# Fused pooled attention and gated feed-forward: the first block's turned probabilities move into buffers of the second tile's x, and the first tile's turns and value products move to other PSUM buffers

## The chip, the cores and the metric

The kernel runs on one core of one Trainium2 chip. The metric is the device time of one execution in microseconds (us). The engines of that core are named as the profile names them: PE does matrix products (PEld loads their stationary operand), DVE, ACT and POOL are the vector, scalar and general engines, and SP issues the transfers. Each engine works through its own list of instructions in the order in which the program gave them, and waits where an operand or a buffer is not ready.

## The reference

Inputs are q, k, v of 8 batches, 8 heads, 576 rows, 64 columns, and three weight matrices of a feed-forward layer with 512 inputs and 1536 inner columns.

```python
k_p = k.reshape(B, H, Sp, 8, D).mean(axis=3)      # 576 keys pooled to 72
v_p = v.reshape(B, H, Sp, 8, D).mean(axis=3)
scores = scale * np.matmul(q, k_p.transpose(0, 1, 3, 2))
scores = scores - np.max(scores, axis=-1, keepdims=True)
attn = np.exp(scores)
attn = attn / (np.sum(attn, axis=-1, keepdims=True) + 1e-09)
attn_out = np.matmul(attn, v_p)
x = attn_out.transpose(0, 2, 1, 3).reshape(B * S, H * D)   # 4608 x 512
a = x @ w_a
b = x @ w_b
return a * b @ w_out
```

The host hands the weights over as 64-bit floating point words, and the kernel turns them into float32 on the chip. Every operand of a product is split into a high and a low part, so that one product is three matmuls (high by high, high by low, low by high).

## The kernel before, in words

**Tiles, chunks and blocks.** The 4608 rows are nine tiles of 512. The attention works in chunks of at most 128 rows that belong to one batch. Chunks 0 to 3 are the first tile (the code calls them first, `i < early`), chunks 4 to 8 are the second tile. Chunks whose value product is made together form a block: chunks 0 and 1 are block 0, chunks 2 and 3 block 1, chunk 4 block 2, chunks 5 and 6 block 3, chunks 7 and 8 block 4.

**One chunk** (`chunk(i)`) goes through these stages, each after the one before: split q into qh and ql; the scores in two groups (`psc`, lines 407 to 424), of which DVE takes the maximum away (lines 401 and 402); the exponential on ACT (451); sum, a small addition and the reciprocal on DVE (453 to 455); the product with the reciprocal on POOL or DVE (457); the split into `pr` and `rem`, whose high part ACT copies (466, 468) and whose low part POOL makes (470, 471); three turns (`turn(0)`, `turn(1)`, `turn(2)`, the transposes of line 502 into `ptr`), each copied by ACT into the tiles p0, p1, p2 (503). The last chunk of a block then makes the value product in two halves (`po`, lines 537 to 546): ACT copies the result to xh (548) and DVE makes xl (550, shown under line 182, as every low part is).

**The feed-forward.** For a tile t and an inner slice f of 128 columns, `ffn_in(t, f)` is 24 matmuls: 12 into `psa` and 12 into `psb`; ACT copies psa to h (606), DVE multiplies it with psb (556), and h is split into hh and hl. `ffn_out(t, f)` is 12 matmuls into the four `acc` tiles. The weights of slice f must have been converted before (`convert_weights`: lines 224 and 225 on ACT, 226, 230 and 235 on DVE, for a, b and o) and split (`split_weight`). The order of slices is written out: in(0,0), in(0,1), out(0,0), in(0,2), out(0,1), in(0,3), out(0,2), in(0,4), in(1,4), out(0,3) and so on: from slice 4 the second tile's products share the first tile's weights.

**What sets the order around the change.** All the work beside the feed-forward consists of generators, the chains, that a small planner (`Chains`) resumes in steps while the program is being written. A chain that yields a number comes back so many steps later; one that yields `PE` joins a queue (`wanting`) and is resumed when it is granted its PE work. A queue entry with a lower rank goes first, and the rank of a chunk is its number. Three things set how fast steps and grants go:

- `need(ready)` runs steps one after the other until a condition holds, with up to 4 grants in each (`GROUPS`), and no matmul of the feed-forward is written between them. At the start it waits for all value products of the first tile and the first weights; before each `ffn_in(t, f)` it waits for `have(t)`, all value products of tile t.
- `ffn_in` makes one step before every 6 matmuls (4 in all) and `ffn_out` one before every 6 (2 in all), each with a single grant. After the first `ffn_in` there is one step more.
- A chain also waits for marks. Chunk i splits its rows into `pr` only after chunk i - 2 is turned; it turns only after chunk i - 1 is turned and the block before its own has its value product, since p0, p1 and p2 exist once (line 505). The scores of chunk i follow `probs` of chunk i - 2, and chunks of the second tile load their q after the scores of chunk i - 2.

The second tile's chunks start at fixed steps (14, 17, 20, 23, 26), whatever the feed-forward does. The conversion of slice f + 1 waits until `ffn_in(0, f - 1)` has begun; that of o starts with the first `ffn_in`.

**PSUM.** The tag `att` has two buffers, `acc` four, `psa` and `psb` one each. In the first tile the scores use `acc`, the turns `att`, the value product of block 0 `psa` and `psb`, and that of block 1 `att`. The scores and turns of the second tile use `att`.

Of the kernel before, what the change touches and what calls it, by code (L numbers as in the profile page):

```python
# [9 lines left out]
F32 = mybir.dt.float32  # L10
F32R = mybir.dt.float32r
# [9 lines left out]
P = 128  # L21
DM = H * D
DF = 1536
NT = 512
NTILE = B * S // NT
NF = DF // P
NK = DM // P
# [25 lines left out]
BLOCK, BLOCK_LATER = 256, 384  # L53
# [26 lines left out]
class Chains:  # L80
# [12 lines left out]
    def wait(self, *marks):  # L93
        while not all(m in self.done for m in marks if not isinstance(m[-1], int) or m[-1] >= 0):
            yield 1
# [26 lines left out]
def attn_moe_kernel(ctx: ExitStack, tc: tile.TileContext, q, k, v, vr, wa, wb, wo, out):  # L122
    nc = tc.nc
    const = ctx.enter_context(tc.tile_pool(name="const", bufs=1))
    sb = ctx.enter_context(tc.tile_pool(name="sb", bufs=2))
    ps = ctx.enter_context(tc.tile_pool(name="ps", bufs=1, space=bass.MemoryType.PSUM))
# [3 lines left out]
    mark, wait, done = chains.mark, chains.wait, chains.done  # L130
# [21 lines left out]
    tile_of = [(b * S + o) // NT for b, o, n in flat]  # L152
# [22 lines left out]
        start = stop  # L175
    block_of = [x for x, block in enumerate(blocks) for _ in block]
    vrems, parts, xtiles, turned, begun, later = {}, {}, {}, {}, [], {}
    upcoming = {name: [] for name in ("a", "b", "o", "h")}
    held = dict.fromkeys(upcoming, 0)

    def low_part(eng, lo, src, hi):
        eng.tensor_tensor(out=lo, in0=src, in1=hi.bitcast(F32), op=ALU.subtract)  # L182
# [188 lines left out]
    def chunk(i):  # L371
        b, o, n = flat[i]
        t, col = divmod(b * S + o, NT)
        first, soon = i < early, t < 2
# [19 lines left out]
        s = sb.tile([P, H, SP], F32, tag="s", name=f"s_{i}")  # L394
# [11 lines left out]
        if i < SUMMED:  # L406
            for g0 in range(0, NK, 2):
                yield from wait(("keys", b, g0))
                yield PE
                if first:  # L410
                    pt = ps.tile([P, 512], F32, tag="acc", name=f"psc_{i}_{g0}", bufs=4)
                else:
                    pt = ps.tile([P, 512], F32, tag="att", name=f"psc_{i}_{g0}", bufs=2)
                for j in range(2):
                    g = g0 + j
# [9 lines left out]
        else:  # L425
            for g in range(NK):
# [3 lines left out]
                pt = ps.tile([P, 512], F32, tag="att", name=f"psc_{i}_{g}", bufs=2)  # L430
# [45 lines left out]
        j = block_of[i]  # L476
# [6 lines left out]
        def turn(x):  # L483
            rows = P if x < 2 else NR
            num = NK if x < 2 else NG
            if x not in turned[j]:
                if tile_of[i] < 2:
                    turned[j][x] = sb.tile([P, num, BLOCK], F32R, tag=f"p{x}", name=f"p{x}_{j}", bufs=1)
                elif x == 0:
                    both = sb.tile([P, 2, NK, BLOCK_LATER], F32R, tag="work", name=f"p_{j}", bufs=1)  # L490
                    turned[j].update({0: both[:, 0], 1: both[:, 1]})
                else:
                    turned[j][x] = sb.tile([P, NK * BLOCK], F32R, tag="p0", name=f"p{x}_{j}", bufs=1)[
                        :, :NG * BLOCK_LATER
                    ].rearrange("p (g s) -> p g s", g=NG)
            dst = turned[j][x]
            pt = ps.tile([P, 512], F32, tag="att", name=f"ptr_{i}_{x}", bufs=2)
            ptr = pt.bitcast(F32R).rearrange("p (g s) -> p g s", g=NK)
            for g in range(num):
                src = pr[:n, x, 2 * g:2 * g + 2, :] if x < 2 else rem[:n, g]  # L500
                src = src.rearrange("p a s -> p (a s)") if x < 2 else src.rearrange("p a c s -> p (a c s)")
                nc.tensor.transpose(ptr[:rows, g, :n], src, ident[:n, :n])  # L502
            nc.scalar.copy(dst[:rows, :, c0:c0 + n], ptr[:rows, :num, :n])

        yield from wait(("turned", i - 1), ("value", j - 1))
        if t >= 2:
            yield from wait(*(("weight", name, NF - 1) for name in ("a", "b", "o")))
        for x in range(3):
            if x < 2 or t < 2:
                yield PE  # L510
            turn(x)
            if x != 1 or t < 2:
                yield 1
# [7 lines left out]
        xh, xl = xtiles[t]  # L521
# [3 lines left out]
        th, tl, tr = (turned[j][x] for x in range(3))  # L525
        for g0 in range(0, NK, per):
            yield PE
            if j == 0:
                po = ps.tile([P, 512], F32, tag="psb" if g0 else "psa", name=f"po_{j}_{g0}")
            else:  # L530
                po = ps.tile([P, 512], F32, tag="att", name=f"po_{j}_{g0}", bufs=2)
            pov = po[:, :per * total].rearrange("p (g s) -> p g s", g=per)
            for g in range(g0, g0 + per):
                if per == NK and g == NK // 2:
                    yield PE
                dst = pov[:, g - g0, :]
                nc.tensor.matmul(dst, vd[:, g, 0, :], th[:, g, :total], start=True, stop=False)
                nc.tensor.matmul(dst, vd[:, g, 0, :], tl[:, g, :total], start=False, stop=False)  # L538
                nc.tensor.matmul(dst, vd[:, g, 1, :], th[:, g, :total], start=False, stop=False)  # L539
                nc.tensor.matmul(  # L540
                    dst,
                    vrem[:NR, g // 2, g % 2].rearrange("p e d -> p (e d)"),
                    tr[:NR, g // 2, :total],
                    start=False,
                    stop=True,
                )
            gs = slice(g0, g0 + per)
            nc.scalar.copy(xh[:, gs, cols], pov)
            yield 1
            low_part(nc.vector, xl[:, gs, cols], pov, xh[:, gs, cols])  # L550
# [58 lines left out]
    acc = {}  # L609
# [52 lines left out]
    for kind, t, f, *_ in order:  # L662
        x = t * NF + f
# [7 lines left out]
    with tc.manual_schedule():  # L671
# [8 lines left out]
        for i in range(early):  # L680
            chains.start(chunk(i), (CHUNKS[0], i), EARLY_GAP * i)
        for i in range(early, sum(t < 2 for t in tile_of)):
            chains.start(chunk(i), (CHUNKS[0], i), SECOND_START + SECOND_GAP * (i - early))
# [15 lines left out]
        for n, (kind, t, f, *_) in enumerate(order):  # L699
            x = t * NF + f  # L700
# [10 lines left out]
        for i in range(len(flat)):  # L711
            b, o, n = flat[i]
            t = tile_of[i]
            if t < 2:
                continue
            since = free if t == 2 else begin_of[t - 1]
            share = (b * S + o + n - t * NT) / NT
            begin_at = since + int((begin_of[t] - since) * share) - CHUNK
            plan.append((begin_at, chunk(i), (CHUNKS[0], i)))
            if i + 1 < len(flat) and flat[i + 1][0] > max(b, 1):  # L720
                plan.append((begin_at - KEYS_AHEAD, load_keys(b + 1), KEYS))
                plan.append((begin_at - KEYS_AHEAD + VALUES_AFTER, load_values(b + 1), KEYS))
# [60 lines left out]
```

## Time and profile before

| what | value |
|---|---|
| median of 3 runs | 1086.49 us (1084.5 to 1088.29) |
| the profiled execution | 1083.36 us |
| its span in the profile | 1081.6 us |
| PE busy, share of the span | 1032.1 us, 95% |
| DVE, ACT, POOL busy | 54%, 48%, 47% |
| granted TensorE clock, mean | 0.984 |

The span is what the profile covers; some 1.8 us of the profiled execution's time lie outside it. A busy share is an average over very different stretches. Rows of the timeline read: start in us, duration in us, engine, line, operation, output<-input, shape, and in brackets the idle time of that engine before the row and who ended it. Rows of the windows read: the stretch, its length, busy time and number of instructions of each engine, the granted clock, the share of the DMA engines and GB/s.

### The profile page before, as it was taken

To read this page: it belongs to the slowest core of one execution; us is meant where nothing else is said; L and a number is where in the kernel's file an instruction comes from. 1 tells how busy PE (TensorE), PEld (TensorE's weight loads), DVE (VectorE), ACT (ScalarE), POOL (GpSimd) and SP (SyncE) were. 2 spreads that over 40 slices of the span, in tenths; PEclk is the share of its full clock that TensorE was granted. 3 is DMA by queue.
4 is the path that set the end of the run, shared out by engine and by line. 5 is a ranking of instruction groups with operands and counts; after the bars stand their busy time and mean duration, and the time that the engine had idled before them with its cause. 6 is when DMAs were issued, how large, how long until landed. Compare 5 with 4: busy or idle time off the path is not lost.

```text
span 1081.6 us, 13576 instructions
## 1 busy us (share of the span) xinstructions
PE 1032.1 (95%) x4964; PEld 855.9 (79%) x4964; DVE 585.9 (54%) x941; ACT 515.6 (48%) x1035; POOL 506.6 (47%) x425
## 2 busy tenths in 40 slices
PE   4569999999999999999999999999999999999998
PEld 4457788788878888888877888888887888888886
DVE  8879967845784347534575437543567344322112
ACT  4656645454554445444544445444543444443332
POOL 6322200055565555555546545554545455554442
PEclk9769999999999999999999999999999999999999
DMA  6335445221330004000320003100220010001001
GB/s 221 105 120 157 147 137 170 93 90 50 115 110 1 1 23 140 14 1 1 96 90 1 1 5 106 45 1 1 93 83 1 1 59 1 1 1 39 1 1 39
DMA packets 32178, 63.79 MB, mean 59 GB/s; under 512 B 7376, under 2 KB 7376, under 8 KB 32112
## 3 DMA queue, kind: packets, MB, share of 16 engines
q1 hardware_dynamic: 32112, 62.93, 18.1%
q8 instruction: 39, 0.64, 0.3%
q14 instruction: 27, 0.22, 0.1%
HBM read 51.38 MB, written 11.53 MB: 58 GB/s over the span
## 4 chain that ended last, share of the span: by engine, by line
PE 85%; DVE 9%; ACT 3%; issue 2%; DMA 1%; POOL 0%; DVEq 0%; ACTq 0%; POOLq 0%
PE psb L599 9%; PE psa L599 9%; PE acc L621 9%; PE psb L601 9%; PE psb L600 8%; PE psa L601 8%; PE psa L600 8%; PE acc L623 8%; PE acc L622 8%; PE ptr L502 2%; PE psc L431 2%; PE psc L417 1%; PE po L539 1%; PE po L540 1%; PE po L538 1%
## 5 line engine op out<-in xcount | busy, mean ns | idle before, releaser
L556 DVE TENSOR_TENSOR h<-psb,h 128x512 f32<-128x512 f32 x108 | 74.6, 691 | 318.7 <-PE psb L601 312.8
L182 POOL TENSOR_TENSOR jlb<-wb_raw,jhb 128x512 fp32r<-128x512 f32 x88 | 115.1, 1307 | 254.6 <-ACT jhb L261 254.6
L182 POOL TENSOR_TENSOR jlo<-wo_raw,jho 128x512 fp32r<-128x512 f32 x108 | 143.1, 1325 | 122.5 <-ACT jho L261 122.5
L606 ACT COPY h<-psa 128x512 f32<-128x512 f32 x108 | 63.5, 588 | 251.8 <-PE psa L601 239.8
L599 PE MATMUL psa<-xh,jha 128*128 128x512 f32 x432 | 173.7, 402 | 0.0
L599 PE MATMUL psb<-xh,jhb 128*128 128x512 f32 x432 | 172.0, 398 | 0.8 <-DVE h L556 0.8
L621 PE MATMUL acc<-jho,hh 128*128 128x512 f32 x432 | 171.6, 397 | 0.0
L600 PE MATMUL psa<-xl,jha 128*128 128x512 f32 x432 | 169.4, 392 | 0.7 <-DVE xl L182 0.7
L601 PE MATMUL psa<-xh,jla 128*128 128x512 f32 x432 | 169.7, 393 | 0.4 <-DVE jla L182 0.4
L601 PE MATMUL psb<-xh,jlb 128*128 128x512 f32 x432 | 168.8, 391 | 0.0
L600 PE MATMUL psb<-xl,jhb 128*128 128x512 f32 x432 | 168.7, 391 | 0.0
L623 PE MATMUL acc<-jho,hl 128*128 128x512 f32 x432 | 168.6, 390 | 0.0
L622 PE MATMUL acc<-jlo,hh 128*128 128x512 f32 x432 | 168.2, 389 | 0.0
L182 POOL TENSOR_TENSOR jla<-wa_raw,jha 128x512 fp32r<-128x512 f32 x88 | 120.6, 1371 | 73.9 <-ACT jha L261 66.6
L182 DVE TENSOR_TENSOR hl<-h,hh 128x512 fp32r<-128x512 f32 x100 | 92.7, 927 | 33.5 <-ACT hh L569 33.3
L569 ACT CAST hh<-h 128x512 fp32r<-128x512 f32 x100 | 62.2, 622 | 95.1 <-DVE h L556 92.5
L601 PEld LDWEIGHTS psa<-xh,jla 128*128 128x128 f32 x432 | 81.8, 189 | 18.5 <-DVE jla L182 0.8
L601 PEld LDWEIGHTS psb<-xh,jlb 128*128 128x128 f32 x432 | 81.2, 188 | 17.4
L623 PEld LDWEIGHTS acc<-jho,hl 128*128 128x128 f32 x432 | 81.1, 188 | 17.5
L599 PEld LDWEIGHTS psb<-xh,jhb 128*128 128x128 f32 x432 | 81.3, 188 | 16.4 <-DVE h L556 1.2
L600 PEld LDWEIGHTS psa<-xl,jha 128*128 128x128 f32 x432 | 82.0, 190 | 15.6 <-DVE xl L182 1.1
L599 PEld LDWEIGHTS psa<-xh,jha 128*128 128x128 f32 x432 | 81.7, 189 | 14.8
(93 smaller groups left out, 1693.4 us busy)
## 6 DMA issues: line engine op xcount, KB each, us to landing
out<-y SPq DMA_DIRECT2D x36, 256.0 KB, 2.2
kraw<-in_k SPq DMA_DIRECT2D x28, 288.0 KB, 4.1
qraw<-in_q SPq DMA_DIRECT2D x28, 256.0 KB, 3.7
vraw<-in_v SPq DMA_DIRECT2D x28, 256.0 KB, 3.1
words<-in_wa SPq DMA_DIRECT2D x12, 512.0 KB, 3.6
words<-in_wb SPq DMA_DIRECT2D x12, 512.0 KB, 3.5
words<-in_wo SPq DMA_DIRECT2D x12, 512.0 KB, 3.6
vraw<-in_vr SPq DMA_DIRECT2D x14, 192.0 KB, 2.6
```

The source lines that it names most:

```text
L182: eng.tensor_tensor(out=lo, in0=src, in1=hi.bitcast(F32), op=ALU.subtract)
L431: nc.tensor.matmul(pt[:n, :2 * hk], qh[:, g, :n], kd[:, g].rearrange("p w e s -> p (w e s)"), start=True, stop=False)
L502: nc.tensor.transpose(ptr[:rows, g, :n], src, ident[:n, :n])
L556: nc.vector.tensor_tensor(out=h, in0=pt, in1=h, op=ALU.mult)
L569: nc.scalar.copy(hh, h)
L599: nc.tensor.matmul(pt, wh[:, c], xh[:, kk], start=(kk == 0), stop=False)
L600: nc.tensor.matmul(pt, wh[:, c], xl[:, kk], start=False, stop=False)
L601: nc.tensor.matmul(pt, wl[:, c], xh[:, kk], start=False, stop=(kk == NK - 1))
L606: nc.scalar.copy(h, pt)
L621: nc.tensor.matmul(acc[c], hh[:, cs], wh, start=first, stop=False)
L622: nc.tensor.matmul(acc[c], hh[:, cs], wl, start=False, stop=False)
L623: nc.tensor.matmul(acc[c], hl[:, cs], wh, start=False, stop=last)
```

## The change

The probabilities of block 0, once turned, lie in a buffer of the tag `xh` (turns 0 and 1, half each) and one of the tag `xl` (turn 2). These tags have two buffers each; the first tile's x takes the other one, and the second tile's x comes later to the buffer that block 0 used. So p0, p1 and p2 are free for block 1, and line 505 no longer waits for the value product of block 0 before chunk 2 turns. Turn 2 of the first tile's chunks goes to `acc` instead of `att`, and the value product of block 1 to `psa` and `psb` instead of `att`.

```diff
+    early_p = {}
...
             if x not in turned[j]:
-                if tile_of[i] < 2:
+                if j == 0:
+
+                    if x != 1:
+                        early_p[x] = sb.tile([P, NK, NT], F32R, tag="xl" if x else "xh", name=f"early_p{x}").rearrange(
+                            "p g s -> p (g s)"
+                        )
+                    turned[j][x] = early_p[x & 2][:, (x & 1) * NK * BLOCK:][:, :num * BLOCK].rearrange(
+                        "p (g s) -> p g s", g=num
+                    )
+                elif tile_of[i] < 2:
                     turned[j][x] = sb.tile([P, num, BLOCK], F32R, tag=f"p{x}", name=f"p{x}_{j}", bufs=1)
...
-            pt = ps.tile([P, 512], F32, tag="att", name=f"ptr_{i}_{x}", bufs=2)
+            tag, bufs = ("acc", 4) if first and x == 2 else ("att", 2)
+            pt = ps.tile([P, 512], F32, tag=tag, name=f"ptr_{i}_{x}", bufs=bufs)
...
-        yield from wait(("turned", i - 1), ("value", j - 1))
+        yield from wait(("turned", i - 1), *([("value", j - 1)] if j > 1 else []))
...
-            if j == 0:
+            if first:
                 po = ps.tile([P, 512], F32, tag="psb" if g0 else "psa", name=f"po_{j}_{g0}")
             else:
                 po = ps.tile([P, 512], F32, tag="att", name=f"po_{j}_{g0}", bufs=2)
```

## The prediction

> **What bounds the kernel now.** I read the page first, then windows around the start, then the timelines of PE, DVE, ACT and POOL up to 130 us, and last the code's planner, counted by hand.
>
> ```profile
> PE 1032.1 (95%) x4964; PEld 855.9 (79%) x4964; DVE 585.9 (54%) x941; ACT 515.6 (48%) x1035; POOL 506.6 (47%) x425
> PE   4569999999999999999999999999999999999998
> 52.60:61.25 8.65, 5.80 (x27) 5.08 (x27) 5.06 (x11) 2.59 (x7) 2.99 (x3) 0.50 0.28 91
> 61.25:128.00 66.75, 57.01 (x277) 43.62 (x276) 62.94 (x106) 47.51 (x96) 16.67 (x13) 0.90 0.48 143
> 128.00:160.00 32.00, 31.97 (x141) 26.45 (x142) 21.32 (x34) 15.20 (x29) 2.59 (x2) 1.00 0.45 140
> ```
>
> PE is the bound from 128 us on: 31.97 of 32.00. Nothing in the change touches that part. So the end moves by as much as PE's arrival there moves, and the question is when PE reaches it, with which work done. Between 61.25 and 128 DVE is the bound (62.94 of 66.75, 3.8 idle): it converts weights for slices 1 to 6 and carries the second tile's attention, while PE has nearly 10 us idle. Just before, between 52.60 and 61.25, no engine is full: a stretch of waits, and it is there that the change acts.
>
> ```profile
> 45.59 0.72 PE L502 MATMUL ptr<-ident,pr 128*128 128x128 f32 x4 [0.85 <-DVE s L402]
> 50.01 0.58 PE L537 MATMUL po<-p,vdiag 128*128 128x256 f32 x1
> 53.38 0.41 PE L540 MATMUL po<-p,vrem 96*128 96x256 f32 x1
> 55.44 0.70 PE L417 MATMUL psc<-kdiag,qh 128*128 128x144 f32 x2 [1.64 <-DVE xl L182]
> 58.20 0.67 PE L502 MATMUL ptr<-ident,pr 64*128 64x64 f32 x4 [1.21 <-DVE s L402]
> 60.90 0.79 PE L599 MATMUL psa<-xh,jha 128*128 128x512 f32 x1
> 50.59 0.45 DVE L402 TENSOR_TENSOR s<-psc,m 64x288 f32<-64x288 f32 x1
> 53.51 1.27 DVE L333 TENSOR_REDUCE vp<-vraw 128x64 f32<-128x512 f32 x2
> 54.70 0.68 DVE L182 TENSOR_TENSOR xl<-po,xh 128x512 fp32r<-128x512 f32 x1
> 57.03 0.46 DVE L401 TENSOR_REDUCE m<-psc 128x4 f32<-128x288 f32 x1 [1.65 <-PE psc L417]
> 57.97 0.68 DVE L182 TENSOR_TENSOR xl<-po,xh 128x512 fp32r<-128x512 f32 x1
> 60.39 0.46 DVE L401 TENSOR_REDUCE m<-psc 128x4 f32<-128x288 f32 x1 [1.74 <-PE psc L417]
> 61.25 0.68 DVE L182 TENSOR_TENSOR ql<-qraw,qh 128x512 fp32r<-128x512 f32 x1
> 58.96 0.37 ACT L503 CAST p<-ptr 128x256 fp32r<-128x256 f32 x1 [2.89 <-PE ptr L502]
> 106.86 0.45 DVE L401 TENSOR_REDUCE m<-psc 128x4 f32<-128x288 f32 x1
> 107.84 0.69 ACT L451 ACTIVATE s<-s 128x576 f32<-128x576 f32 x1 [0.57 <-DVE s L402]
> 110.35 0.74 DVE L453 TENSOR_REDUCE z<-s 128x8 f32<-128x576 f32 x1
> 111.34 0.20 DVE L455 RECIPROCAL z<-z 128x8 f32<-128x8 f32 x1
> ```
>
> The 16 value matmuls of block 1 run from 50.01 to 53.8. Then the `att` pair is handed around: chunk 6's scores wait for xl to free a buffer, DVE waits for those scores, chunk 4's turn waits for DVE, and only behind all that, at 60.90, stands the first matmul of the feed-forward. The last four rows are chunk 8's, later, and give prices: 0.98 from the start of its last maximum to its exponential, and 1.19 from the start of its sum to the end of the reciprocal (110.35 to 111.54).
>
> **The change part by part.** (1) *PSUM of turn 2.* The four turn-2 tiles of the first tile leave `att`. Nothing is added; PE's waits for a copy or for s (0.85 at 45.59) shrink. DVE was busy through that time, so I cost this at nothing; if DVE were not the cover it would be worth those waits, under 1 us each.
>
> (2) *Block 0 in buffers of x, no wait for its value product.* In planner steps, before: chunk 1 is turned at step 15, chunk 2 turns at 18 to 20, chunk 3 at 21 to 23, block 1's value product at 25 and 26, marked at 27, and the feed-forward begins with step 28. After: chunk 2 turns at 15 to 17, chunk 3 at 18 to 20, value product at 22 and 23, marked at 24; the feed-forward begins with step 25. ACT's p copies move ahead of the conversion of b on its queue, which delays DVE by an estimated 0.3 (about one short copy, 0.37 at 58.96). No DMA is added, and the loads on SP keep their steps. The buffers themselves cost nothing: the second tile's x asks for its buffer only at step 31, long after block 0's last matmul.
>
> (3) *Block 1's value product in psa and psb.* It no longer holds `att`. The first feed-forward matmul now has to wait until DVE has made xl from psa, but its neighbours need that xl anyway: nothing.
>
> *The start, in time.* Before, DVE ended the last scores of chunk 5 at 51.04 (50.59 + 0.45). After, it does the same, 0.3 later, and behind them only the two xl of 0.68: 52.7. PE has by then only block 1's value product and chunk 5's scores behind it, and the first feed-forward matmul comes at about 52, some 9 us before 60.90. Taken alone that looks like a large gain. It is not, for DVE has not done what it had done at 61.25: one sum-and-reciprocal (1.19), one ql (0.68), two vp (1.27) and two max-and-subtract pairs (0.98 each) are still to come: 5.1 us. So DVE's lead is 61.25 - 52.7 - 5.1 = 3.5 us (rounded up).
>
> *What is queued behind the earlier start.* In the feed-forward each step has one grant, and the lowest chunk goes first. Before, chunk 6's two score groups were granted at steps 26 and 27, inside `need` with its four grants. After, step 25 is already the feed-forward's. Chunk 4 takes grants 26, 27, 28 for turns and 30, 31 for values, chunk 5 takes 32 to 34; chunk 6's score groups get 29 and 35 (before 26 and 27). Everything behind hangs on it: chunk 8 loads its q after chunk 6's scores and makes its scores after chunk 6's probs. Counted on: chunk 6 turns at 41 to 43, its value product 45 and 46; chunk 7 turns 47 to 49; chunk 8's last score group comes at 50 (before 42), exponential 51, sum 52, product 53, split 54 and 55, turns 56 to 58, value product 60 and 61, marked at 62 (before 55). But in(0,4) is through after step 51, and in(1,4) needs that mark: `need` runs steps 52 to 62, where before it ran one. In them no feed-forward matmul is written, and PE stands waiting for one chunk's serial chain:
>
> ```profile
> 111.68 1.16 POOL L457 TENSOR_TENSOR s<-s,z 128x576 f32<-128x576 f32 x1 [5.17 <-ACT h L606]
> 112.87 0.62 ACT L466 CAST pr<-s 128x512 fp32r<-128x512 f32 x1 [1.25 <-POOL s L457]
> 113.57 1.81 POOL L182 TENSOR_TENSOR pr<-s,pr 128x512 fp32r<-128x512 f32 x1 [0.73 <-ACT pr L466]
> 115.33 0.78 POOL L182 TENSOR_TENSOR rem<-s,rem 128x64 fp32r<-128x64 f32 x1
> 117.47 0.31 PE L502 MATMUL ptr<-ident,rem 128*96 128x128 f32 x2
> 120.73 0.35 ACT L503 CAST p<-ptr 96x256 fp32r<-96x256 f32 x1
> 119.40 0.68 DVE L230 SCALAR_TENSOR_TENSOR wo_raw<-words,wo_raw 128x512 int32<-128x512 int32 x1
> 120.22 0.69 DVE L235 CUSTOM_DVE_ANT_0 wo_raw<-wo_raw,wlow_o 128x1024 uint16<-128x1024 uint16 x1
> 117.61 0.46 PE L599 MATMUL psa<-xh,jha 128*128 128x512 f32 x1
> 119.76 0.39 PE L599 MATMUL psa<-xh,jha 128*128 128x512 f32 x1
> 125.58 0.39 PE L599 MATMUL psa<-xh,jha 128*128 128x512 f32 x1
> 127.29 0.68 DVE L182 TENSOR_TENSOR xl<-po,xh 128x512 fp32r<-128x512 f32 x1
> 128.03 0.50 PE L600 MATMUL psa<-xl,jha 128*128 128x512 f32 x1 [0.68 <-DVE xl L182]
> ```
>
> The first eight are chunk 8's own rows before (from the product to the copy of its last turn), with feed-forward matmuls between the stages. Before, in(1,4) starts at 125.58 and loses 0.68 once to xl, so it counts as 126.26.
>
> *When chunk 8's last maximum starts, after (X).* DVE begins the shared work at 52.7 and has to do what it did from 61.25 to 128 (62.94), the 5.1 moved in, without what comes after that maximum: the pair itself 0.98, the rest of b's conversion 1.37 (0.68 + 0.69), one h (taken as 0.68, like xl), a sum 1.19, two xl 1.36, together 5.6. 52.7 + 62.94 + 5.1 - 5.6 = 115.1 with no idle at all; with the 3.8 idle of before, 118.9. I take 118.9, since the same waits between DVE, ACT and loads are there; 115 to 121 are the ends.
>
> *From X to in(1,4).* Maximum to exponential 0.98, exponential 0.69, sum to reciprocal 1.19, product 1.16, split 0.62, low parts 1.81 and 0.78, turn 0.31, its copy 0.35: 7.9. Then 16 value matmuls, at half clock as at 50.01 to 53.38 (15 starts in 3.37, 0.225 each): 3.6. Some nine hand-overs at 0.05 to 0.1: 0.7. Sum 12.2; ends 10.5 (low parts without company, value product at full clock) and 14 (ACT and DVE queues in the way). PE's tail of in(0,4), 12 matmuls, lies beside the first 3 us. So in(1,4) starts at 118.9 + 12.2 = 131.1, 4.8 later than 126.26.
>
> *The clock.*
>
> ```profile
> 80.11 0.67 PE L502 MATMUL ptr<-ident,pr 64*128 64x64 f32 x4 [4.46 <-DVE xl L182]
> 80.70 0.79 PE L599 MATMUL psa<-xh,jha 128*128 128x512 f32 x1
> 85.32 0.44 PE L599 MATMUL psb<-xh,jhb 128*128 128x512 f32 x1
> ```
>
> After 4.46 idle, the ten feed-forward matmuls from 80.70 to 85.32 took 4.6, less 0.3 for a turn; at full speed (117.61 to 119.76, nine starts, 0.239 each) ten take 2.4: a cost of 1.9. In `need` PE has about 3 us of nothing, then short turns, copies and values. I take 1.6, with 0 and 1.9 as ends. [...]
>
> *Sum.* -9 at the start turns into 4.8 late at in(1,4), plus 1.6: +6.4 on the profiled execution's 1083.36, 1089.8. That execution lies 3.1 under the median 1086.49 and under all three runs, so the same sum on the median is 1092.9; since the next runs may fall nearer the lower end of 1084.5 to 1088.29, I give 1092.
>
> **The rivals.** *The lead is kept (faster).* The second tile's values are marked before they are needed, or the chain hides behind the tail of in(0,4); then DVE's order alone sets the end: 118.9 + 5.6 = 124.5 for the last xl instead of 127.97, so 3.5 less, 1083; with no idle 7.3 less, 1079. For it: DVE is the bound for 67 us, and a lead there is real. Against: 11 steps of `need`. It decides where chunk 8's last scores come by step 43 or so. 0.14.
>
> *A wash.* X = 115 to 117 because the densely packed conversions leave DVE no idle, a chain of 11, the clock kept: in(1,4) at 126 to 128, 0 to 2 later, 1086 to 1089. For it: POOL is mostly idle and `need` gives four grants. 0.24.
>
> *PE becomes slow itself.* Started early, PE waits for conversions slice by slice; with gaps like the 4.46 again and again it stays at half clock. The 156 matmuls up to in(1,4) take 37 at 0.239 and 72 at 0.46; if half of them are slow, 18 are added. PE's slack from 52 to 122 is 70 - 37 less some 16 for the second tile's share (57.01 busy before, less 37 and the slow matmuls), about 17, so that a part shows beside the chain: +8 to +14, 1095 to 1100. For it: the half clock at 80 to 85. Against: DVE is late in any case, and slow matmuls beside it cost nothing. 0.1.
>
> **How the numbers follow.** Forecast 0.52, its own range 1089 to 1096. About 0.3% (3.3 us) is what a measurement can tell from no change. Faster takes most of the first rival: 0.14; same is the wash: 0.25; slower the forecast and the slow PE, less their low edge: 0.61. The range leaves out the outer half of the first rival and the top of the last: 1082 to 1098.
>
> **What the profile after would show.** First L599 matmul at 51 to 54 instead of 60.90; chunk 6's score groups (128*128 psc) behind it; a gap of PE of 6 us or more, broken by chunk 8's turns and values, ahead of the first in(1,4); that matmul near 131; PE's clock at half around it; from there PE full as before. The forecast is wrong if in(1,4) starts before 126, or if a pause of that kind is absent.

## The result: slower by 1.1%, and the profile after

| what | before | after |
|---|---|---|
| median, same chip | 1086.63 us, 4 runs (1084.5 to 1088.29) | 1097.95 us, 4 runs (1095.66 to 1099.94) |
| the profiled execution, its span | 1083.36, 1081.6 | 1099.94, 1098.2 |
| first feed-forward matmul, in(0,0) | 60.90 | 52.60 |
| in(0,4) | 117.61 | 120.71 |
| in(1,4) | 125.58 | 139.56 |
| out(0,3) | 132.06 | 146.13 |

The profiled execution of the changed kernel is the highest of its four, and that of the kernel before lies under all four of its runs: the two spans differ by 16.6 us where the medians differ by 11.3. The ratio of the times is 1.0108, with an interval of 1.0087 to 1.0129. (Ratios are given as recorded; they are not quotients of the medians, and differ from those by up to 0.13%.) From the turns on, lines stand 11 further down in the changed kernel (502 became 513, 599 became 610); lines ahead of them stand one further down (182 became 183).

First the engines' row of the page of the changed kernel, and PE's row of its 40 slices.

```profile
PE 1036.8 (94%) x4964; PEld 860.6 (78%) x4964; DVE 588.3 (54%) x941; ACT 516.3 (47%) x1035; POOL 505.7 (46%) x425
PE   4577699999999999999999999999999999999998
```

The work is the same in number: every engine has as many instructions as before. Slice 3 is a little fuller than before (7 tenths for 6), slices 4 and 5 (82 to 137 us) are lighter (7 and 6 tenths for 9 and 9), and everything after them is as full as it was. PE's timeline shows what the light slices are made of.

```profile
52.60 0.79 PE L610 MATMUL psa<-xh,jha 128*128 128x512 f32 x1 [0.77 <-DVE xl L183]
66.07 0.45 PE L418 MATMUL psc<-kdiag,qh 128*128 128x144 f32 x2 [4.28 <-ACT p L514]
92.13 0.41 PE L418 MATMUL psc<-kdiag,qh 128*128 128x144 f32 x2 [3.24 <-DVE s L403]
102.62 0.75 PE L513 MATMUL ptr<-ident,pr 128*128 128x128 f32 x4 [4.09 <-ACT pr L467]
120.71 0.47 PE L610 MATMUL psa<-xh,jha 128*128 128x512 f32 x1
132.70 0.75 PE L513 MATMUL ptr<-ident,pr 128*128 128x128 f32 x4 [5.39 <-ACT pr L467]
134.55 0.75 PE L513 MATMUL ptr<-ident,pr 128*128 128x128 f32 x4 [1.10 <-POOL pr L183]
139.56 0.63 PE L610 MATMUL psa<-xh,jha 128*128 128x512 f32 x1
142.03 0.40 PE L610 MATMUL psa<-xh,jha 128*128 128x512 f32 x1
```

The feed-forward starts 8.3 us earlier, as forecast, and chunk 6's scores come behind it, at 66.07. At 92.13 and 102.62 PE waits for the second tile again, first for scores of chunk 7 that DVE holds up, then for a turn of chunk 6 that ACT holds up. Then comes the pause: from the end of in(0,4) at 127.31 (132.70 less the 5.39 of waiting) to in(1,4) at 139.56 PE does only chunk 8's turns and 16 value matmuls.

### The profile page after: what moved, and what is told of

Same layout as the page of the kernel before. It is cut to its first block, busy times and chain, and to the rows that moved or that the text cites. A ratio compares the mean times of both kernels' runs of the same rounds, so it can differ in the third digit from the quotient of the medians.

```text
span 1098.2 us, 13575 instructions
## 1 busy us (share of the span) xinstructions
PE 1036.8 (94%) x4964; PEld 860.6 (78%) x4964; DVE 588.3 (54%) x941; ACT 516.3 (47%) x1035; POOL 505.7 (46%) x425
## 4 chain that ended last, share of the span: by engine, by line
PE 81%; DVE 11%; ACT 3%; DMA 3%; issue 2%; POOL 0%; SPq 0%; DVEq 0%; ACTq 0%; POOLq 0%
PE psa L610 8%; PE acc L632 8%; PE psb L610 8%; PE acc L634 8%; PE acc L633 8%; PE psa L612 8%; PE psa L611 8%; PE psb L612 8%; PE psb L611 8%; PE ptr L513 2%; PE psc L432 2%; DVE vp L334 1%; PE po L550 1%; PE po L548 1%; PE po L551 1%
```

## The experiments

All times are medians, and every ratio is against the kernel before on the same chip. Rows and windows are of one execution of each kernel. Theory A, from the prediction: the earlier start takes grants away from the second tile's chunks, the last of them is late, and `need` stops the feed-forward. The rivals: the buffers or PSUM cost it; or (theory B) the early start itself does, by packing conversions where no other work stands between them.

### Which part of the change it is

**The wait put back, buffers and PSUM as changed.**

```diff
-        yield from wait(("turned", i - 1), *([("value", j - 1)] if j > 1 else []))
+        yield from wait(("turned", i - 1), ("value", j - 1))
```

> The kernel after, with the wait for block 0's value product put back for chunk 2; buffers of x and PSUM tiles as after. The planner's steps are those of before (values of the second tile at 55). Theory of the grants: the time of before, 1085 to 1088, with at most 1 us gained by the looser att pair. Rival (buffers or PSUM tiles): 1094 or more.

Measured: 1083.5, ratio 0.9977 (0.9959 to 0.9995), a little under the expected range.

**PSUM put back, the wait away.** Turn 2 and block 1's value product go to `att` again.

> The kernel after without its PSUM part: turn 2 and block 1's value product back in att, the wait still taken away. Steps as after (values at 62, eleven steps of waiting). Theory of the grants: 1095 to 1100, like after, perhaps 1 to 2 us more because turns, scores and values share two buffers again. Rival (the PSUM tiles make the loss): 1088 or less.

Measured: 1098.64, ratio 1.0102 (1.008 to 1.0124), as slow as the whole change. So neither the buffers nor PSUM are the cause: all the loss comes with the wait that was dropped.

**The feed-forward held until step 28**, where it began before, all else as changed.

```diff
-        need(lambda: have(0) and all((n, 0) in parts for n in ("a", "b")))
+        need(lambda: chains.now >= 28 and have(0) and all((n, 0) in parts for n in ("a", "b")))
```

> The kernel after, with the feed-forward held back until planner step 28, where it began before. Block 1's values are still marked at 24; chunk 6's scores fall inside the first wait (27), the second tile's values come at 54, one or two steps of waiting. Theory of the grants: the loss is gone, 1083 to 1087, a little under before since the first tile's stretch is denser. Rival (the conversions that come with an early start are the cost, not the grants): also about 1086; so this run tells both from the rival of the buffers and PSUM tiles (1094 or more), and run e1 tells the two apart.

Measured: 1083.55, ratio 0.9981 (0.9965 to 0.9997). in(0,0) comes at 60.36 and in(1,4) at 124.92. The attention of the first tile is as early as in the change; only the start is late, and the loss is gone.

### How the loss goes with the step of the start

> The kernel after, with the feed-forward held until planner step 26 (after: 25, the run that held it until 28 took 1083.6). Counted in the code, the one grant of step 26 still goes to chunk 4's turn: chunk 6's scores at 35, the second tile's values at 62, ten steps of waiting ahead of in(1,4). Theory of the grants: nothing is won, 1095 to 1099. Rival (every step that the feed-forward begins earlier costs its share, through the conversions that begin with it): a third of the way, 1092 to 1095.

> The kernel after, with the feed-forward held until planner step 27: chunk 6's first score group now falls inside the first wait, its second is granted at 29; values at 56, three steps of waiting ahead of in(1,4). Theory of the grants: most of the loss goes at once, 1083 to 1088, so that nearly all of the difference between 25 and 28 lies between 26 and 27. Rival (a share per step): two thirds of the way, 1087 to 1091.

> The kernel after, held until planner step 30, two steps later than before's start. The second tile goes as in the run held until 28; no step of waiting stands ahead of in(1,4). If the time depends on how far the feed-forward's conversions stand ahead of the second tile's work in the queues (theory B), the trend of 1098, 1096, 1090.5, 1083.6 for steps 25 to 28 goes on a little or levels: 1080 to 1084. If only the grants matter (theory A), two more steps of an idle PE cost 1 to 3 us: 1084 to 1087.

| held until step | none (25) | 26 | 27 | 28 | 30 |
|---|---|---|---|---|---|
| ratio | 1.0108 | 1.0106 | 1.0045 | 0.9981 | 0.9992 |
| in(0,0) | 52.60 | 51.60 | 56.98 | 60.36 | 63.62 |
| in(1,4) | 139.56 | 136.41 | 128.68 | 124.92 | 126.41 |

(Intervals for 26, 27 and 30: 1.0081 to 1.0131, 1.0027 to 1.0063, 0.9978 to 1.0007.) The later the feed-forward starts, up to step 28, the earlier it has the second tile. But the series doesn't separate A from B, since both grow with the early start. At step 27, where I expected nearly nothing left, 0.45% remained, which the rival's reading foresaw; at step 30 the 1085.77 lies in A's range and above B's, but steps 28 and 30 differ by less than their intervals.

### Grants alone

**Two grants in each step of the whole feed-forward of tile 0** (`chains.step(2)`), the start early.

> The kernel after, with two grants instead of one in each step that the feed-forward of the first tile makes. Counted in the code, chunk 6's scores are then through at step 27 (after: 35), chunk 8's at 34 (50), and the second tile's values are marked at 49 (62), while in(0,4) ends with step 51: no wait stands ahead of in(1,4). Theory (the queue of grants makes the second tile late, and that alone costs the time): the pause of PE ahead of in(1,4) is gone, the first feed-forward matmul stays near 52 us, in(1,4) starts at 122 to 125, and the time is 1082 to 1086. Rival (the buffers of x or the PSUM tiles of the turns cost the time themselves): 1094 or more. Rival (DVE's idle among the early conversions costs it, whatever the grants): DVE still idles 8 us or more between the first tile's last xl and in(1,4), 1088 to 1092.

Measured: 1089.98, ratio 1.0037 (1.0023 to 1.0051). A miss: I had counted only the grants that were lacking. The last rival of this expectation, DVE's idle, had both the time and the idle right: DVE idles 12.9 us between the first tile's last xl (53.28) and in(1,4) (132.17). The windows of that kernel (length, then PE, PEld, DVE, ACT, POOL busy, then PE's clock):

```profile
51.89:110.00 58.11, 41.79 (x176) 32.75 (x177) 51.99 (x88) 33.01 (x69) 16.71 (x16) 0.76 0.42 123
110.00:132.17 22.17, 22.17 (x116) 18.43 (x115) 15.38 (x26) 16.25 (x31) 2.60 (x2) 0.98 0.44 136
```

There is no pause now: PE is full for the last 22 us before in(1,4), and 6.8 of DVE's idle lies there, where it costs nothing. But up to 110 DVE carries the second tile's attention beside the conversions (51.99 busy of 58.11), PE is busy for only 41.79, and in(0,3) is at 115.50 instead of 106.51 before. As I read it, the attention has been moved too far forward.

**The second tile's chunks started three steps earlier** (steps 11 to 23 instead of 14 to 26), and **score groups granted ahead of turns and values**:

> The kernel after, with the second tile's chunks started three planner steps earlier (11 instead of 14), so that chunk 6's scores come inside the first wait though the feed-forward begins at step 25: values of the second tile at 53, two steps of waiting ahead of in(1,4). Theory of the grants: 1080 to 1086; in(1,4) begins before 126. The first feed-forward matmul comes 1 to 3 us later than in after, since DVE has chunk 6's scores first. Rival (an early start costs in any case, as with two grants, 1090): 1088 to 1092.

> The kernel after, with score groups granted ahead of turns and value products whatever the chunk. Chunk 6's scores are through at 25, chunk 8's at 34, block 1's values at 28, so that the feed-forward begins with step 29; the second tile's values come at 55 and in(1,4) waits for none of them. Theory A: 1082 to 1086. Theory B: also, since the feed-forward begins late, 1081 to 1086. If it is 1088 or more, the scores' work on DVE ahead of the first products costs more than either says.

Measured: 1093.94, ratio 1.0069 (1.0044 to 1.0094), and 1094.44, ratio 1.0078 (1.006 to 1.0095). Two misses, and as I read them of the same kind. In the second the feed-forward begins only at 63.54 and in(1,4) comes at 135.43: this order loses without an early start, which neither A nor B foresaw. (The profiled execution of the first, 1088.86, is the fastest of six and 5 under their median.) These are PE's longest waits behind the start in the two, both for work of the second tile:

```profile
78.06 0.67 PE L513 MATMUL ptr<-ident,pr 64*128 64x64 f32 x4 [6.00 <-ACT p L514]
```

```profile
86.51 0.39 PE L548 MATMUL po<-p,vdiag 128*128 128x64 f32 x1 [5.65 <-DVE s L403]
```

**The extra grants only where they were lost**: in `ffn_in`, at steps 25 to 27. The second tile's work then falls in the same steps as with the start held, and the feed-forward still begins at step 25.

```diff
-                    chains.step()
+                    chains.step(2 if chains.now < 28 else 1)
```

> The kernel after, with two grants only in steps 25 to 27, those that lie between its start of the feed-forward and that of before. Every chunk of the second tile then goes at the same steps as in the run that held the feed-forward until 28 (1083.6): chunk 6's scores 27, values 41 and 54. All that differs from that run is that the feed-forward and its conversions begin three steps earlier; three steps of waiting stand ahead of in(1,4) instead of one or two. Theory A (only the order of grants costs): 1082 to 1086. Theory B (an early start of the feed-forward costs by itself, since its conversions stand on DVE and ACT ahead of the second tile's work, about 5 us as with two grants throughout, 1090, and with the second tile's chunks three steps earlier, 1089 to 1094): 1088 to 1092.

Measured: 1085.35, ratio 0.9994 (0.9983 to 1.0006): three grants take the whole loss away. Rows of its PE, and then its window from in(0,0) to in(1,4):

```profile
51.58 0.80 PE L610 MATMUL psa<-xh,jha 128*128 128x512 f32 x1 [0.77 <-DVE xl L183]
62.69 0.67 PE L418 MATMUL psc<-kdiag,qh 128*128 128x144 f32 x2 [4.92 <-DVE s L403]
82.03 0.57 PE L513 MATMUL ptr<-ident,pr 64*128 64x64 f32 x4 [3.88 <-DVE xl L183]
125.07 0.47 PE L610 MATMUL psa<-xh,jha 128*128 128x512 f32 x1
```

```profile
51.58:125.07 73.49, 58.52 (x290) 45.94 (x291) 66.50 (x114) 49.17 (x100) 19.16 (x18) 0.91 0.46 138
```

This is the run that decides between A and B as they were written down: the start is as early as in the change (51.58), so B's loss should have stayed (1088 to 1092), and it did not. It doesn't tell apart the ways in which missing grants can cost, a late chain ahead of in(1,4) or conversions with nothing between them, since the three grants undo both. It also shows what the early start is worth by itself: nothing that these runs can tell. With the start held until step 28, the same stretch is this:

```profile
60.36:124.92 64.56, 53.10 (x269) 42.06 (x269) 58.90 (x103) 46.40 (x93) 16.77 (x13) 0.93 0.47 142
```

It begins 8.8 us later and ends at the same time. DVE is busy for 66.50 of 73.49 in the one and 58.90 of 64.56 in the other, and from the start of the program to in(1,4) it has 192 instructions in both. Of PE's 8.9 us more, 3.5 are more idle (14.97 against 11.46; the early start waits 4.92 and 3.88 for DVE in two rows), and 5.4 are more busy time, with 21 instructions more and a clock of 0.91 against 0.93.

### Two that bear on the pause and on the conversions

**The second tile one slice later** (`LAG` 4 to 5, so that in(1,5) is the first to need it):

> The kernel after, with the second tile joining at slice 5 instead of 4 (36 feed-forward matmuls more, some 8.4 us, are written ahead of the first product that needs the second tile; slice 4 of the second tile is done later instead). Values still at 62, five steps of waiting ahead of in(1,5). If the pause ahead of the second tile's first product is the cost (12.7 us from the end of in(0,4) to in(1,4) in the trace), it shrinks to 3 to 6 us and the time is 1087 to 1093; if PE's waits behind chunk 6's scores and turns before it are the greater part, it stays above 1093.

Measured: 1092.73, ratio 1.0066 (1.0042 to 1.0091). Nearly all of the pause is bridged (from chunk 8's last maximum at 124.36 to in(1,5) at 139.98 PE is busy for 13.56 of 15.62), and 0.66% remains. So the pause is not the whole loss, unless joining a slice later costs something by itself, which no run shows. PE's long waits ahead of it are still there, 5.93 at 64.87 for chunk 6's scores and 4.12 at 100.78 for its turn; this run doesn't show what they cost by themselves.

**Conversions three steps later**, the start early:

> The kernel after, with the conversions of every weight after slice 0 begun three planner steps later than after (at the steps of before), the feed-forward's first products at 52 us as in after. Slice 1's weights are then late, the wait for them runs steps with four grants, and chunk 6's scores come at 30, the second tile's values at 57; in(1,4) starts at step 58. Theory B (the early conversions cost, not the early products): 1083 to 1088. Theory A (grants): three steps of waiting as in the run held until 27 (1090.5), 1087 to 1091.

Measured: 1091.99, ratio 1.0055 (1.0037 to 1.0073), in(1,4) at 130.03. Half of the loss is gone, which lies above B's range by 4 us and above A's by 1. The run doesn't tell what the conversions are worth alone, for it moved grants too: by the count chunk 6's last scores come at step 30 instead of 35, and the second tile's values at 57 instead of 62.

## Why the prediction was right in kind and too small

The forecast was 1092, slower; it came out slower at 1097.95, 6 above. The change cost 11.3 us by the medians where 5.5 were forecast, twice as much. The time lies outside the 1089 to 1096 that the forecast itself allowed; that the whole range ended at 1098 and holds it by 0.05 us is luck. The sum was made on profiled executions, where it said +6.4 and +16.6 was measured; 5.3 of these 16.6 are how far the two executions lie from their medians, and the terms below are to be read with that. The mechanism stood at each place that it named: the first matmul at 52.60 (forecast about 52), chunk 6's scores behind it, a pause ahead of in(1,4) broken by chunk 8's turns and values, half clock around it (0.53 granted from 139.56 to 142.03), PE full afterwards (30.00 of 30.00 from 145.00). The step that failed is a term of the sum: **X, when chunk 8's last maximum starts**, put at 118.9 and measured at 126.63, and in it DVE's idle time, which the forecast took over from the kernel before. These are the rows of the changed kernel's DVE, ACT and POOL that it is read from.

```profile
47.37 0.67 DVE L183 TENSOR_TENSOR jlb<-wb_raw,jhb 128x512 fp32r<-128x512 f32 x1
53.32 0.67 DVE L183 TENSOR_TENSOR xl<-po,xh 128x512 fp32r<-128x512 f32 x1
65.24 0.50 DVE L227 TENSOR_SCALAR wb_raw<-wb_raw 128x512 int32<-128x512 int32 x1 [2.58 <-ACT wb_raw L225]
81.20 0.43 DVE L227 TENSOR_SCALAR wo_raw<-wo_raw 128x512 int32<-128x512 int32 x1 [1.74 <-ACT wo_raw L225]
125.65 1.06 DVE L227 TENSOR_SCALAR wb_raw<-wb_raw 128x512 int32<-128x512 int32 x1 [1.96 <-ACT wb_raw L225]
126.63 0.44 DVE L402 TENSOR_REDUCE m<-psc 128x4 f32<-128x288 f32 x1
62.69 0.62 ACT L262 CAST jha<-wa_raw 128x512 fp32r<-128x512 f32 x1 [1.94 <-DVE wa_raw L236]
64.55 0.66 ACT L225 ACTIVATE wb_raw<-words 128x512 f32<-128x512 f32 x1
80.50 0.67 ACT L225 ACTIVATE wo_raw<-words 128x512 f32<-128x512 f32 x1 [2.94 <-DMA words<-in_wo]
127.60 0.68 ACT L452 ACTIVATE s<-s 128x576 f32<-128x576 f32 x1 [1.44 <-DVE s L403]
130.84 1.15 POOL L458 TENSOR_TENSOR s<-s,z 128x576 f32<-128x576 f32 x1 [4.42 <-DVE z L456]
132.72 1.77 POOL L183 TENSOR_TENSOR pr<-s,pr 128x512 fp32r<-128x512 f32 x1 [0.73 <-ACT pr L467]
```

The windows on both sides of X, and one after the pause:

```profile
54.00:126.63 72.63, 56.81 (x260) 44.21 (x259) 61.58 (x104) 44.88 (x90) 15.85 (x13) 0.86 0.47 140
126.63:139.56 12.93, 6.19 (x30) 5.19 (x29) 8.70 (x14) 5.35 (x11) 3.66 (x3) 0.69 0.27 81
145.00:175.00 30.00, 30.00 (x134) 24.85 (x133) 19.36 (x31) 14.22 (x26) 2.59 (x2) 1.00 0.39 123
```

And one row of the kernel before, the same instruction as the first above:

```profile
45.37 0.67 DVE L182 TENSOR_TENSOR jlb<-wb_raw,jhb 128x512 fp32r<-128x512 f32 x1
```

Term by term:

- *Early lists.* An instruction that the change doesn't touch stands at 47.37 instead of 45.37. With the same early order, other experiments had their first feed-forward matmul at 51.43 to 52.92, so much of these 2.0 is likely the difference of two executions. With them the last xl of the first tile ends at 54.00 instead of the forecast 52.7: 1.3 of X's 7.7.
- *DVE's work to X.* Forecast 62.94 + 5.1 - 5.6 = 62.4 from the last xl; measured 61.58, 0.8 less. The counting of moved work was right.
- *DVE's idle to X.* Taken over from before as 3.8; measured 72.63 - 61.58 = 11.05. This is the failure: 7.25, and 1.3 - 0.8 + 7.25 is X's 7.7. Three rows carry 6.28 of it: DVE waits for ACT's half of a conversion (2.58, 1.74, 1.96). ACT is late for another reason each time: at 64.55 it comes from a row of casts, begun at 62.69, most of them the second tile's; at 80.50 it has waited 2.94 for words from a DMA; at 124.95 a copy of psa and a cast (from 123.94) stand ahead. The forecast moved the work correctly and kept the idle time of another arrangement. As I read it, the second tile's attention filled such holes before, and had here been put off to `need`; no run shows this by itself.
- *That idle in other runs.* The run with three extra grants bears the reading out in part: between in(0,0) and in(1,4) DVE is idle for 15.3 us in the changed kernel (86.96 - 71.64), 7.0 with the three grants (73.49 - 66.50) and 3.8 before (65.36 - 61.55, to 126.26). So over half goes with the grants, and some 3 us come with the early start though no grant is missing. Two other kernels in which the grants are as late show how far the size holds. With the old PSUM the idle to X (126.91) is 10.76. Held until step 26 it is only 6.47 and X is at 120.57, but DVE's wait for b's conversion comes right behind X instead (2.51 at 124.03): X to in(1,4) takes 15.84 there, and the loss is the same.
- *From X to in(1,4).* Forecast 12.2, measured 12.93. Its hand-overs were put at 0.05 to 0.1; two rows of the kernel before have 0.03 (POOL's product to ACT's copy at 112.87) and 0.08 (that copy to POOL at 113.57). The rows 126.63, 127.60, 130.84, 132.72 and 135.98 to 139.35 (16 value matmuls) are the chain that was priced from chunk 8's own rows.
- *The clock.* Forecast 1.6, an estimate that no run shows; its upper end was the 1.9 that the kernel before lost after 4.46 of idle. In the changed kernel the first six matmuls from 139.56 to 142.03 took 2.47 at a granted clock of 0.53, where full speed at 0.239 is 1.43: 1.0.
- *After the pause.* Forecast nothing; out(0,3) is 14.07 late, the end 16.6. The 2.5 between are told below; 1.5 of them is a step of the clock that the run with the old PSUM doesn't have.

Of the rivals, *the lead is kept* would have needed chunk 8's scores by step 43, and they came at step 50, as counted. That rival exists, though: the run with three extra grants is it, and the 3.5 us of DVE's lead that it priced did not appear (0.9994): DVE's idle rose from 3.8 to 7.0, nearly what the lead had been. *PE becomes slow itself* named the time that was measured, but not its way: PE was busy 56.81 for 260 instructions up to X, against 57.01 for 277 before, 0.22 instead of 0.21 each, not half of 156 matmuls at 0.46. *A wash* is what the run with three extra grants reaches in its time, but not with a DVE that has no idle.

The best two, the wait put back and the start held until step 28, are 0.2% under the kernel before, with intervals that end just below 1. That is less than the 0.3% that this measurement was said to tell.

**What stays open.** It is not known why 0.45% remains when the start is held until step 27, where by the count chunk 6's second score group is only two steps late and `need` runs three. It is not a pause such as A names, for from 113 us to in(1,4) PE has no wait of more than 0.3. The longest waits of that run are 6.08 at 76.33 and 3.52 at 112.73, both ahead of turns (the second is chunk 7's), and what they cost was not taken apart. And with the later conversions 0.55% remains where A had 0.1 to 0.45%; which part of that is theirs was not taken apart either.

## What to carry to other kernels

An earlier start is worth what the engine that bounds the stretch behind it gains, not what the starting engine gains: with the three grants put back PE began 8.8 us sooner than with the start held, and DVE, busy for 9 tenths of the next 70 us, had nothing sooner to give. Where a program is written out in steps with a limited number of grants, an earlier start also changes who gets the next grants: count, step by step, when the last piece of the other work is granted and who waits for it. And when work is moved out of a stretch, the idle time of that stretch must be worked out anew: the moved work may have been what filled it.

## What the runs showed of the clock

The same wait can cost the clock or not. These rows are PE's of the kernel before, and then of the changed kernel, at the same point of the program (a turn that waits for `s`):

```profile
310.72 0.51 PE L502 MATMUL ptr<-ident,pr 128*128 128x128 f32 x4 [1.88 <-DVE s L437]
311.83 0.40 PE L599 MATMUL psa<-xh,jha 128*128 128x512 f32 x1
```

```profile
325.52 0.50 PE L513 MATMUL ptr<-ident,pr 128*128 128x128 f32 x4 [1.86 <-DVE s L438]
326.95 0.63 PE L610 MATMUL psa<-xh,jha 128*128 128x512 f32 x1
```

Idle 1.88, and the matmuls go on at 0.40 (granted clock 1.00 from 311.83 to 314.83); idle 1.86, and they take 0.63 for most of the next 3 us (0.55 from 326.95 to 329.95), which put the changed kernel back by 1.5 us against the one before. The same happened with a wait of over 3 us: 3.24 at 92.13 left the changed kernel's clock full (0.41), and the same wait of 3.22 in the run with the old PSUM halved it:

```profile
92.44 0.67 PE L418 MATMUL psc<-kdiag,qh 128*128 128x144 f32 x2 [3.22 <-DVE s L403]
```

Behind it the feed-forward matmuls from 94.29 to 97.70 start 0.43 apart; behind the 3.24 those of the changed kernel from 93.11 to 96.78 start 0.23 apart. So the length of a wait doesn't decide by itself: after 1.86 us of idle at 325.52 the clock fell, and after 3.24 at 92.13 it did not. What decides is not shown by these runs. When the feed-forward matmuls are counted back from the last one, the changed kernel's are 14.1 late at 190 us, 14.7 at 220, 16.3 at 334 and 16.9 from 591 on; one such step is the half clock at 326, the others stand at longer waits near 213 (1.38 for 0.76 before) and 577 (2.17 for 1.41). The run with the old PSUM is 14.1 late at 220 and 13.9 at 1077, without such a step in between. The run held until step 28 is 1.7 early at 190 and 3.8 late at 591: its turn that waits 1.86 at 311.23 lost the clock too (0.63 for each matmul from 311.90 to 313.61), and the execution that was profiled is the slowest of its ten (1087.19, the fastest 1081.68). Steps of 1 to 2 us that fall or do not fall in one execution are likely a good part of the 4 us between the changed kernel's four runs, though only one of these was profiled.
